# Splitting one attention mix around the next unit's logits in a gated attention and feed-forward kernel

## The chip, the core and the metric

The kernel runs on one core of a Trainium2 chip. The core has a matrix engine (TensorE, PE in the profile; its weight loads are PEld), a vector engine (VectorE, DVE), a scalar engine (ScalarE, ACT), a general engine (GpSimd, POOL) and a queue engine (SyncE, SP), and transfers (DMA) that SP, ACT and POOL issue. The metric is the time of one execution on the device in microseconds (us). Before the change three runs gave 593.22, 592.76 and 597.3 us, a median of 593.22.

## The reference

For 2048 tokens of 512 channels the kernel computes a gate g per token, an attention a, a feed-forward b, and g * a + (1 - g) * b. The attention has 32 heads of 16 channels; each token looks at 8 earlier ones, 2 apart.

```python
def _A_ref(x, wqkv, wo):
    H = 32; Dh = D // H; W, dil = 8, 2
    q, k, v = ...                       # x @ wqkv, by head
    idx = pos[:, None] - arange(W) * dil
    logits = einsum("bhsd,bhswd->bhsw", q, kg) * Dh ** -0.5   # masked where idx < 0
    attn = softmax(logits, axis=-1)
    o = einsum("bhsw,bhswd->bhsd", attn, vg)
    return o @ wo

def _B_ref(x, w_gate, w_up, w_down):
    return (gelu(x @ w_gate) * (x @ w_up)) @ w_down

g = sigmoid((x * gate_w).sum(-1, keepdims=True))
return g * a + (1 - g) * b
```

## The kernel before, in words

As the window has a step of 2, even and odd tokens never meet. The kernel does the even half (the first parity, `par` 0) and then the odd half (the second parity, `par` 1). For each parity it makes keys and queries, then values, and runs the feed-forward in 14 stages `f` (`ffn`, `gate_up`, `down`). All products are made on TensorE in single precision from pairs of a high and a low part, with block products saved by sums of operands (seven products in place of eight).

**Attention** is not on TensorE. A unit is 128 of the 512 channels (8 heads) of one parity, so there are four units for each parity, (0,0) to (0,3) and (1,0) to (1,3). For each unit VectorE does:
- `scores`: four times a product of queries and keys (tile `prod` from `kq`, L539) and its sum over a head's channels (L542) into the logits `lg`;
- `exps`: the maximum (L553), a subtraction (L555), and the exponential on ScalarE (L557);
- `shares`: the sum (L562), its reciprocal (L564), for the second parity the gate (L566), and a product (L568);
- `mix`: four times a product of the shares with the values (tile `v`, L585) and three additions (L589, L591, L593) into `o`, and after each second one a transposition (L598) into `tb`, whose four stores go to the DRAM tile `os` (L600, on SP).

**Loads.** `load_kq` fetches the keys and queries of a unit into the one buffer `kq`, `load_values` the values into the one buffer `v`, both on SP (L520, L523, L524). A load waits until the last product that reads the buffer is done.

**What sets the order.** `attention` is a generator that yields a number, an estimate of VectorE time, after each piece of work. The feed-forward calls `pull` with a budget between its products, and `pull` takes pieces off the generator until the budget is used. The pieces get a lower priority (`BEHIND`), and a scheduler then sets the final order of every engine's instructions, which the engines take in order. So a change to the order of pieces can move the instructions of all engines from that point on. From the fifth unit on (`i >= PIPE`, the second parity) the units are pipelined: between a unit's shares and its mix stand the next unit's logits and exponential.

**Feed-forward helpers on VectorE and ScalarE.** In each stage ScalarE copies products out of the banks `p` and `acc` of the accumulator memory (L786, L792, L845, L882, L898) and puts earlier sums back (L824, L867); VectorE adds (L793), multiplies (L797) and makes the low parts `hl` (L801). Four `p` banks serve in turn, so a product waits until its bank has been copied out.

**The end.** `out_first` multiplies the first parity's attention by the output weights (L1062, tile names `p_5354` and later). `finish` adds the second parity's: `channels` loads `os` into `raw` (L1040, SP), ScalarE casts the high part `hh` (L90), VectorE subtracts to make the low part `hl` (L91), TensorE adds the products for 4 units and 8 row groups (L1062) into `acc` and `p`, and copies on ScalarE (L1111) and VectorE (L1109) go to the output (L1115). The last pair is `hh_5673` and `hl_5674`.

Of the kernel before, what the change touches and what calls it, by code (L numbers as in the profile page):

```python
# [36 lines left out]
PIPE = 4  # L37
# [11 lines left out]
def tile_gated_mix(ctx: ExitStack, tc: tile.TileContext, xt, wqkv, wff, wo, out):  # L49
# [458 lines left out]
    def load_kq(par, u):  # L508
        hh, c = divmod(u, 2)
        kq = KQ.pop() if KQ else pool.tile([P, 3 * NP - 1, UC], F32, name="kq")  # L510
        k, q = kq[:, :2 * NP - 1], kq[:, 2 * NP - 1:]
        LG[par, u] = k, q
        if not (par or u):

            nc.gpsimd.memset(k[:1, :NP - 1], 0.0)
            for a, b in (1, P - 15), (P - 15, P):
                nc.sync.dma_start(k[a:b, :NP - 1], k[a - 1:b - 1, NP:])
            return
        load_slots(k, KS[par, hh][c], paced)
        paced(nc.sync.dma_start(q, QS[par, hh][c].rearrange("(p j) d -> p j d", j=NP)))  # L520
# [50 lines left out]
    VT = {}  # L571

    def load_values(par, u):
        hh, c = divmod(u, 2)
        VT[par, u] = v = pool.tile([P, 2 * NP - 1, UC], F32, name="v")
        load_slots(v, VS[par, hh][c])

    def mix(par, u):
        lg, v = LG.pop((par, u)), VT.pop((par, u))
        tb = pool.tile([P, 2, BT * UC], F32, name="tb")  # L580
        for jj in range(0, NP, 2):
            if jj % BT == 0:
                o = pool.tile([P, 4, BT, 32], F32, name="o")
            prod = pool.tile([P, 2, W, UC], F32, name="prod")
            paced(nc.vector.tensor_tensor(prod.rearrange("p j w (h d) -> p (j w) h d", d=DH),  # L585
                                          spans(v, jj).rearrange("p j w (h d) -> p j w h d", d=DH),
                                          two_of(lg, jj)[:, :, :, None].to_broadcast([P, 2 * W, UH, DH]), op=OP.mult))
            yield 2.3
            nc.vector.tensor_tensor(prod[:, :, :4], prod[:, :, :4], prod[:, :, 4:], op=OP.add)  # L589
            yield 1.2  # L590
            nc.vector.tensor_tensor(prod[:, :, :2], prod[:, :, :2], prod[:, :, 2:4], op=OP.add)  # L591
            two = [prod[:, :, i].rearrange("p j (b c) -> p b j c", b=4) for i in range(2)]
            nc.vector.tensor_tensor(o[:, :, jj % BT:jj % BT + 2], *two, op=OP.add)  # L593
            yield 1.1

            if jj % BT == BT - 2:
                t = tb[:, jj // BT]
                nc.vector.transpose(t, o.rearrange("p b t c -> p (b t c)"))  # L598
                for a in range(4):
                    nc.sync.dma_start(OS[par, u, jj // BT][:, :, a].rearrange("b i c -> i b c"),  # L600
                                      t[32 * a:32 * a + 32].rearrange("p (b c) -> p b c", b=4))
                yield 0.7

    done = set()
# [17 lines left out]
    def attention():  # L622
        units = [(0, u) for u in range(NU)] + [(1, u) for u in range(NU)]
        scored, ready, shared = [0], [], []

        def keyed(i):
            return i < len(units) and (units[i][0], units[i][1] // 2 * 2) in done

        def logits(i):
            if units[i] not in LG:  # L630
                load_kq(*units[i])
                yield LOAD
            yield from scores(*units[i])
            scored.append(i)

        yield from need(0, 0)
        yield from scores(0, 0)
        yield from need(0, 1)
        mixed = False
        for i, un in enumerate(units):  # L640
            if i not in scored:
                yield from need(un[0], un[1] // 2 * 2)
                yield from logits(i)
                mixed = False
            if i not in ready:
                if i >= PIPE and keyed(i + 1):
                    load_kq(*units[i + 1])
                yield from exps(*un)
            yield from need(un[0], 1)
            if i not in shared:  # L650
                yield from shares(*un)
            pipe, ahead = i >= PIPE and keyed(i + 1), i and keyed(i + 1)
            if not pipe and ahead:
                load_kq(*units[i + 1])
            load_values(*un)
            if pipe:
                yield from logits(i + 1)
                if keyed(i + 2):
                    load_kq(*units[i + 2])
                yield from exps(*units[i + 1])  # L660
                ready.append(i + 1)
            elif mixed:
                yield LOAD
            yield from mix(*un)
            done.add((*un, "o"))
            mixed = not ahead
            if pipe:
                yield from shares(*units[i + 1])
                shared.append(i + 1)
            elif ahead:  # L670
                yield from logits(i + 1)
# [684 lines left out]
```

## Time and profile before

| what | value |
|---|---|
| three times | 593.22, 592.76, 597.3 us |
| profiled execution, its own time | 592.89 us |
| its span, first to last instruction | 591.1 us |
| TensorE busy | 585.7 us (99%) |
| VectorE busy | 535.0 us (91%) |
| ScalarE busy | 425.3 us (72%) |
| granted TensorE clock, mean | 1.000 |

A row of the timeline has the start in us from the start of the span, the duration, the engine, the line, the operation, the tile written and the tile read, and in brackets the idle time ahead of it and what ended that. SPq is SP's queue: such a row is the issue of a transfer, not the transfer. A row of stretches has the stretch, its length, and the busy time and count of PE, PEld, DVE, ACT and POOL, then the granted clock, the share of the DMA engines and GB/s. A wait has the waiting instruction, what it waited for, the total, the count and the longest.

### The profile page before, as it was taken

What the parts mean: (1) busy time and instruction counts of PE and PEld (TensorE: products, weight loads), DVE (VectorE), ACT (ScalarE), POOL (GpSimd) and SP (SyncE); (2) the same over time, 40 slices, a digit from 0 to 9 for tenths busy, and PEclk for the clock granted to TensorE, in tenths of its full rate; (3) what the DMA queues carried; (4) which work ended last, traced back from release to release, by engine and by line L of the source; (5) the groups of instructions that cost most, each with busy time, mean ns of one, the idle gap of its engine ahead of it and who ended that gap; (6) DMA issues with size and microseconds to landing.
All of it is one profiled execution on the core that took longest, in us unless ns stands there. A gap on an engine that the chain in (4) does not pass through costs nothing.

```text
span 591.1 us, 8266 instructions
## 1 busy us (share of the span) xinstructions
PE 585.7 (99%) x2743; PEld 489.1 (83%) x2743; DVE 535.0 (91%) x628; ACT 425.3 (72%) x752; POOL 126.8 (21%) x153
## 2 busy tenths in 40 slices
PE   9999999999999999999999999999999999999997
PEld 7889888888888888888889888888888888887885
DVE  6989998999899995998997999998999899989882
ACT  6778667778887779786687655768776967796522
POOL 0140751112111212113120761112121212112200
PEclk9999999999999999999999999999999999999999
DMA  8789999978987979899989999969798989548915
GB/s 305 228 247 281 301 310 231 296 197 238 289 222 218 273 205 273 224 264 347 284 231 380 222 272 269 277 162 257 178 263 224 254 213 247 144 111 227 202 44 178
DMA packets 87848, 141.71 MB, mean 240 GB/s; under 512 B 8575, under 2 KB 49919, under 8 KB 87806
## 3 DMA queue, kind: packets, MB, share of 16 engines
q1 hardware_dynamic: 65454, 103.21, 52.2%
q0 software_dynamic: 22064, 37.59, 34.6%
q8 instruction: 21, 0.34, 0.2%
q10 hardware_dynamic: 288, 0.39, 0.2%
q14 instruction: 21, 0.17, 0.1%
HBM read 69.83 MB, written 46.49 MB: 197 GB/s over the span
## 4 chain that ended last, share of the span: by engine, by line
PE 96%; ACT 2%; DMA 1%; issue 0%; SPq 0%; DVE 0%; ACTq 0%
PE p L781 44%; PE p L830 13%; PE acc L830 12%; PE acc L478 11%; PE p L1062 6%; PE p L364 4%; PE acc L364 3%; PE p L478 2%; PE acc L1062 2%; DMA raw<-xt 1%; ACT A L90 0%; ACT L898 0%; ACT g L135 0%; ACT hl L805 0%; ACT hh L807 0%
## 5 line engine op out<-in xcount | busy, mean ns | idle before, releaser
L781 PE MATMUL p<-S,g 128*128 128x512 f32 x672 | 167.0, 389 | 0.0
L781 PEld LDWEIGHTS p<-S,g 128*128 128x128 f32 x672 | 125.8, 188 | 25.8
L781 PE MATMUL p<-A,g 128*128 128x512 f32 x504 | 125.8, 389 | 0.0
L781 PEld LDWEIGHTS p<-A,g 128*128 128x128 f32 x504 | 94.4, 188 | 19.8 <-ACT rt L845 0.4
L585 DVE TENSOR_TENSOR prod<-v,lg 128x2048 f32<-128x2048 f32 x32 | 72.8, 2274 | 1.4 <-DMA v<-vs 1.2
L542 DVE TENSOR_REDUCE lg<-prod 128x128 f32<-128x2048 f32 x32 | 73.0, 2280 | 0.2
L539 DVE TENSOR_TENSOR prod<-kq 128x2048 f32<-128x2048 f32 x32 | 72.9, 2277 | 0.2
L830 PE MATMUL p<-d,hh 128*128 128x512 f32 x224 | 68.6, 390 | 0.3 <-ACT p L824 0.3
L830 PE MATMUL acc<-d,hh 128*128 128x512 f32 x224 | 59.7, 389 | 0.0
L740 POOL DMA_DIRECT2D g<-raw x26 | 23.6, 907 | 161.1 <-ACT g L737 103.6
L792 ACT ACTIVATE c<-p 128x512 f32<-128x512 f32 x56 | 33.4, 597 | 33.7 <-PE p L781 33.6
L830 PEld LDWEIGHTS p<-d,hh 128*128 128x128 f32 x224 | 41.9, 188 | 9.5 <-ACT p L824 0.8
L830 PEld LDWEIGHTS acc<-d,hh 128*128 128x128 f32 x224 | 42.0, 188 | 8.7
L793 DVE TENSOR_TENSOR c<-c,s 128x512 f32<-128x512 f32 x56 | 37.8, 681 | 5.5 <-ACT c L792 5.2
L830 PE MATMUL p<-d,hl 128*128 128x512 f32 x112 | 42.1, 389 | 0.0
L797 DVE TENSOR_TENSOR c<-c 128x512 f32<-128x512 f32 x56 | 38.1, 683 | 1.3 <-ACT c L898 1.2
L589 DVE TENSOR_TENSOR prod<-prod 128x1024 f32<-128x1024 f32 x32 | 39.0, 1217 | 0.1
L845 ACT ACTIVATE rt<-p 128x512 f32<-128x512 f32 x48 | 27.8, 596 | 15.0 <-PE p L830 14.8
L786 ACT ACTIVATE s<-p 128x512 f32<-128x512 f32 x56 | 33.2, 594 | 5.3 <-PE p L781 4.9
L478 PE MATMUL acc<-d,S 128*128 128x512 f32 x144 | 35.5, 390 | 0.1
L830 PE MATMUL acc<-d,hl 128*128 128x512 f32 x112 | 35.1, 389 | 0.0
L772 POOL DMA_DIRECT2D d<-r x23 | 19.8, 860 | 68.9 <-ACT d L771 41.6
(222 smaller groups left out, 1062.3 us busy)
## 6 DMA issues: line engine op xcount, KB each, us to landing
g<-raw POOLq DMA_DIRECT2D x26, 512.0 KB, 6.7
ws<-g SPq DMA_DIRECT2D x14, 768.0 KB, 5.9
g<-ws SPq DMA_DIRECT2D x14, 768.0 KB, 6.7
r<-wff SPq DMA_DIRECT2D x28, 256.0 KB, 4.4
raw<-wff SPq DMA_DIRECT2D x14, 512.0 KB, 4.6
d<-r POOLq DMA_DIRECT2D x23, 256.0 KB, 6.7
ws<-raw SPq DMA_DIRECT2D x14, 384.0 KB, 5.8
raw<-ws SPq DMA_DIRECT2D x14, 384.0 KB, 4.0
```

The source lines that it names most:

```text
L364: LAST[:] = [nc.tensor.matmul(ps[:, :n], x[:, ts], VO[b][w][:, kc * WQ:kc * WQ + n], start=first, stop=(kc == 1 and i == 2), skip_group_ch ...
L478: LAST[:] = [nc.tensor.matmul(ps, x[:, ts], w, start=(start and kc == i == 0), stop=(kc == 1 and i == 2), skip_group_check=True)]
L539: paced(nc.vector.tensor_tensor(prod, spans(k, jj), q[:, jj:jj + 2, None, :].to_broadcast([P, 2, W, UC]), op=OP.mult))
L542: nc.vector.tensor_reduce(two_of(lg, jj), prod.rearrange("p j w (h d) -> p (j w) h d", d=DH), axis=AX.X, op=OP.add)
L585: paced(nc.vector.tensor_tensor(prod.rearrange("p j w (h d) -> p (j w) h d", d=DH), spans(v, jj).rearrange("p j w (h d) -> p j w h d", d=D ...
L589: nc.vector.tensor_tensor(prod[:, :, :4], prod[:, :, :4], prod[:, :, 4:], op=OP.add)
L781: LAST[:] = [nc.tensor.matmul(ps, w_, a_, start=(start and kc == 0 and n == 0), stop=(kc == 1 and n == 2), skip_group_check=True)]
L792: nc.scalar.activation(c, ps, AF.Copy)
L793: nc.vector.tensor_tensor(c, c, s, op=OP.add)
L797: nc.vector.tensor_tensor(ge, ge, up, op=OP.mult)
L830: LAST[:] = [nc.tensor.matmul(pp, a[:, ts], w, start=(i == 0 and n == 0 and gr == 0), stop=(i == 1 and n == 2), skip_group_check=True)]
L1062: LAST[:] = [nc.tensor.matmul(pa, a, b, start=(first and n == 0), stop=(last and n == 2), skip_group_check=True)]
```

## The change

In `mix`, each of the four quarters is entered in the set `done` once its additions are made. In `attention`, for the first unit of the second parity (`i == PIPE`), the mix is begun ahead of the next unit's logits, and stopped when its second quarter is done; the rest of it (the first transposition with its stores, the third and fourth quarter) follows behind the next unit's logits and exponential, where the whole mix stood. `load_values` of that unit is called ahead of `load_kq` of the next, and ahead of the unit's own exponential. The other units go as before. Nothing that is computed changes.

```diff
--- before.py
+++ after.py
@@ -591,6 +591,7 @@
             nc.vector.tensor_tensor(prod[:, :, :2], prod[:, :, :2], prod[:, :, 2:4], op=OP.add)
             two = [prod[:, :, i].rearrange("p j (b c) -> p b j c", b=4) for i in range(2)]
             nc.vector.tensor_tensor(o[:, :, jj % BT:jj % BT + 2], *two, op=OP.add)
+            done.add((par, u, jj))
             yield 1.1
 
             if jj % BT == BT - 2:
@@ -644,6 +645,7 @@
                 mixed = False
             if i not in ready:
                 if i >= PIPE and keyed(i + 1):
+                    load_values(*un)
                     load_kq(*units[i + 1])
                 yield from exps(*un)
             yield from need(un[0], 1)
@@ -652,8 +654,15 @@
             pipe, ahead = i >= PIPE and keyed(i + 1), i and keyed(i + 1)
             if not pipe and ahead:
                 load_kq(*units[i + 1])
-            load_values(*un)
+            if un not in VT:
+                load_values(*un)
+            steps = mix(*un)
             if pipe:
+                if i == PIPE:
+                    for c in steps:
+                        yield c
+                        if (*un, 2) in done:
+                            break
                 yield from logits(i + 1)
                 if keyed(i + 2):
                     load_kq(*units[i + 2])
@@ -661,7 +670,7 @@
                 ready.append(i + 1)
             elif mixed:
                 yield LOAD
-            yield from mix(*un)
+            yield from steps
             done.add((*un, "o"))
             mixed = not ahead
             if pipe:
```

Lines of the changed kernel from L594 on are 1 higher, and from L673 on 9 higher, than those of before (L793 becomes L802, L1109 becomes L1118).

VectorE, at the softmax of unit (1,0), before (`kq` is the keys of unit (1,1), `c` and `hl` belong to the feed-forward):

```order
L555 TENSOR_TENSOR lg<-lg,m 128x512
L539 TENSOR_TENSOR prod<-kq 128x2048
L562 TENSOR_REDUCE m<-lg 128x64
L542 TENSOR_REDUCE lg<-prod 128x16x8
L793 TENSOR_TENSOR c<-c,s 128x512
L564 RECIPROCAL m<-m 128x64
L793 TENSOR_TENSOR c<-c,s 128x512
L539 TENSOR_TENSOR prod<-kq 128x2048
L797 TENSOR_TENSOR c<-c 128x512
L566 TENSOR_TENSOR m<-m,g 128x64
L542 TENSOR_REDUCE lg<-prod 128x16x8
L797 TENSOR_TENSOR c<-c 128x512
```

VectorE at the same place, after the change:

```order
L555 TENSOR_TENSOR lg<-lg,m 128x512
L562 TENSOR_REDUCE m<-lg 128x64
L564 RECIPROCAL m<-m 128x64
L566 TENSOR_TENSOR m<-m,g 128x64
L568 TENSOR_TENSOR lg<-lg,m 128x512
L802 TENSOR_TENSOR c<-c,s 128x512
L585 TENSOR_TENSOR prod<-v,lg 128x2048
L806 TENSOR_TENSOR c<-c 128x512
L802 TENSOR_TENSOR c<-c,s 128x512
L589 TENSOR_TENSOR prod<-prod 128x2x512
L810 TENSOR_TENSOR hl<-c,hh 128x512
L591 TENSOR_TENSOR prod<-prod 128x2x256
```

The products of the next unit's logits (L539) and their sums (L542) have moved out; the sum of the softmax (L562) follows the subtraction (L555) directly, and the first product of the mix (L585) comes up.

TensorE in the last feed-forward stage, before (`p_5179` is a product of that stage, `p_5289` and `p_5324` take the last but one group of down products, `p_5354` is the first final product of `out_first`; `p_5354` has the bank that `p_5204`, another product of the stage, had):

```order
L830 MATMUL p_5289<-d_4827,hh_4963 128x512 x2
L830 MATMUL p_5289<-d_4827,hl_4964 128x512
L830 MATMUL p_5289<-d_4949,hh_5094 128x512 x2
L830 MATMUL p_5289<-d_4949,hl_5095 128x512
L781 MATMUL p_5179<-S_2942,g1_5106 128x512 x3
L781 MATMUL p_5179<-S_2957,g1_5106 128x512 x3
L830 MATMUL p_5324<-d_4827,hh_4963 128x512 x2
L830 MATMUL p_5324<-d_4827,hl_4964 128x512
L830 MATMUL p_5324<-d_4949,hh_5094 128x512 x2
L830 MATMUL p_5324<-d_4949,hl_5095 128x512
L1062 MATMUL p_5354<-g1_5191,A_5261 128x512 x3
L1062 MATMUL p_5354<-g1_5191,A_5282 128x512 x3
```

TensorE at the same place, after the change:

```order
L790 MATMUL p_5179<-S_2942,g1_5106 128x512 x3
L790 MATMUL p_5179<-S_2957,g1_5106 128x512 x3
L839 MATMUL p_5289<-d_4827,hh_4963 128x512 x2
L839 MATMUL p_5289<-d_4827,hl_4964 128x512
L839 MATMUL p_5289<-d_4949,hh_5094 128x512 x2
L839 MATMUL p_5289<-d_4949,hl_5095 128x512
L1071 MATMUL p_5354<-g1_5191,A_5261 128x512 x3
L1071 MATMUL p_5354<-g1_5191,A_5282 128x512 x3
L1071 MATMUL p_5354<-S_5237,A_5319 128x512 x2
L839 MATMUL p_5324<-d_4827,hh_4963 128x512 x2
```

The product into `p_5179` has moved ahead of `p_5289`, and most of `p_5354` ahead of `p_5324`. On ScalarE, at the same place, the copy that empties `p_5204` (into `c_5279`, L792, now L801) stood behind the one that fills `p_5324` (L824, now L833) and now stands ahead of it.

VectorE at the end of the program, before (`os`, `raw` and `hh_5673` carry the last attention output; `acc1`, `acc3`, `p_5571` and `p_5589` are final sums):

```order
L593 TENSOR_TENSOR o_5394<-prod_5416 128x4x64
L598 STREAM_TRANSPOSE tb_5301<-o_5394 128x512
L91 TENSOR_TENSOR hl_5674<-raw_5632,hh_5673 128x4x4x32
L1109 COPY rt_5704<-acc1_3744 128x512
L1109 COPY rt_5722<-acc3_3746 128x512
L1109 COPY rt_5734<-p_5571 128x512
L1107 COPY rt_5746<-p_5589 128x256
```

VectorE at the end, after the change:

```order
L593 TENSOR_TENSOR o_5394<-prod_5416 128x4x64
L599 STREAM_TRANSPOSE tb_5301<-o_5394 128x512
L1118 COPY rt_5704<-acc1_3747 128x512
L1118 COPY rt_5722<-acc3_3749 128x512
L91 TENSOR_TENSOR hl_5674<-raw_5632,hh_5673 128x4x4x32
L1118 COPY rt_5734<-p_5571 128x512
L1116 COPY rt_5746<-p_5589 128x256
```

The last subtraction L91, which makes `hl_5674`, stood ahead of the copies of `acc1` and `acc3` and now stands behind them. In SP's queue the last load of `raw` stood right behind the last stores of `os`; now the first output transfer (L1115, now L1124) stands between them. On ScalarE the copy of `acc2` stood behind the last cast L90 and now stands ahead of it.

## The prediction

> **What bounds the kernel now.** I read the page first, then who TensorE (PE) waits for, then stretches of the span, then the order of instructions in time around the moved work and at the end.
>
> ```profile
> span 591.1 us, 8266 instructions
> PE 585.7 (99%) x2743; PEld 489.1 (83%) x2743; DVE 535.0 (91%) x628; ACT 425.3 (72%) x752; POOL 126.8 (21%) x153
> ```
> ```profile
> PE p L76 <- DVE warm L73: 1.0, 1, 1.0
> PE p L830 <- ACT p L824: 0.3, 1, 0.3
> ```
> ```profile
> 380.00:576.00 196.00, 195.67 (x863) 161.70 (x862) 184.02 (x194) 140.92 (x235) 32.92 (x39) 1.00 0.77 195
> 576.00:592.00 16.00, 11.28 (x50) 9.01 (x48) 3.10 (x5) 3.41 (x6) 0.00 (x0) 0.99 0.46 164
> ```
>
> The page gives PE 99% of the span: 591.1 - 585.7 = 5.4 us idle in all. The waits of PE name two, 1.0 us at the start and 0.33 us once in the middle. From 380 to 576 us, where the changed work lies, PE is busy 195.67 of 196.00 us; VectorE (DVE), which carries the attention, is busy 184.02, so it has 12.0 us to spare there, and ScalarE (ACT) 55. Most of PE's other idle time is the last stretch, after its last matmul. So the change can give PE nothing beyond that 0.33 us; it can only give it new waits. DVE's time is worth something only where PE waits for it.
>
> That "99%" could hide slow matmuls, so I look at their spacing.
>
> ```profile
> 528.00 1.52 PE L781 MATMUL p<-S,g 128*128 128x512 f32 x6
> 529.36 0.62 PE L830 MATMUL p<-d,hh 128*128 128x512 f32 x2
> L781 PEld LDWEIGHTS p<-S,g 128*128 128x128 f32 x672 | 125.8, 188 | 25.8
> ```
>
> Six matmuls of 512 columns start within 529.36 - 528.00 = 1.36 us, 0.227 us apart, and a weight load takes 0.188 us, so 0.188/0.227 = 83% loading is what a PE without gaps shows here. The Trainium skill ("Perfetto Trace Analysis", Identifying the Most-Contended Engine) says that matmul busy time is a poor measure of the distance to the limit and that the weight loads' share should be read; by that rule 17% would be open. The rows above answer it: the 83% belongs to the shape.
>
> **The change part by part.** Computed work is the same: the same 628 DVE instructions, matmuls and DMAs. Only places move.
>
> *The values' load.* It is written ahead of the second unit's keys, but in SyncE's (SP's) queue it stood there before.
>
> ```profile
> 342.33 0.38 SPq L523 DMA_DIRECT2D v<-vs  x1
> 369.32 0.32 SPq L523 DMA_DIRECT2D kq<-ks  x1
> ```
> ```profile
> 403.67 2.27 DVE L585 TENSOR_TENSOR prod<-v,lg 128x2048 f32<-128x2048 f32 x1
> ```
>
> The values left at 342 us, the keys at 369, and the changed program has both at the same rows of SP. The values are now needed some 23 us before their first product at 403.67, at about 381 us, still over 30 us after their issue. Cost 0.
>
> *The first exponential.* Half of the mix now stands behind the unit's softmax without logits between.
>
> ```profile
> 376.28 0.68 DVE L555 TENSOR_TENSOR lg<-lg,m 128x512 f32<-128x512 f32 x1
> 376.88 2.29 DVE L539 TENSOR_TENSOR prod<-kq 128x2048 f32<-128x2048 f32 x1
> 379.08 0.68 DVE L562 TENSOR_REDUCE m<-lg 128x64 f32<-128x512 f32 x1
> ```
> ```profile
> 377.79 0.63 ACT L557 ACTIVATE lg<-lg 128x512 f32<-128x512 f32 x1
> ```
>
> Before, one product of logits (2.29 us) filled the time that the exponential needs on ACT. Now the sum L562 stands right behind L555: DVE waits from 376.28 + 0.68 = 376.96 to 377.79 + 0.63 = 378.42, **+1.5 us** of DVE.
>
> *The second exponential* gains what the first loses:
>
> ```profile
> 411.55 0.69 DVE L562 TENSOR_REDUCE m<-lg 128x64 f32<-128x512 f32 x1 [2.22 <-ACT lg L557]
> 465.58 0.69 DVE L562 TENSOR_REDUCE m<-lg 128x64 f32<-128x512 f32 x1 [1.66 <-ACT lg L557]
> ```
>
> In the changed order a 2.3 us product of the mix and two 0.68 us additions stand between L555 and L562, beside the two short additions that were there. The 2.22 us wait goes, **-2.2 us**. The third and fourth keep about the same company as before (0).
>
> *The feed-forward's vector instructions.* Summing the attention rows ahead of the same feed-forward row in both orders, at 0.5 to 2.2 us each, gives 0 to 4.9 us less ahead of it in the changed order, nowhere more than 0.4 us more until the last rows. So PE's own helpers on DVE (L793, L797, L801) come earlier and hold PE up nowhere; but DVE's queue is taken in order, and where such a row comes before its operand from ACT, DVE waits and the attention behind it slips. Bounds: nothing (PE's pace leaves the 12.0 us) and 4.9 us (the whole distance waited out once). I take **+2 us**, since the waits of this kind that before shows are 0.3 to 1 us each and a few are added. DVE ends the attention later by d = 1.5 - 2.2 + 2 = 1.3 us, between -0.7 and 4.2. The last transposition has room for that, see below.
>
> *The stores of the first half mix* now stand in SP's queue ahead of a load of r and of a weight load:
>
> ```profile
> 397.32 0.33 SPq L702 DMA_DIRECT2D r<-wff  x1
> 404.38 0.64 ACT L771 ACTIVATE d<-r 128x512 fp32r<-128x512 f32 x1
> ```
> ```profile
> r<-wff SPq DMA_DIRECT2D x28, 256.0 KB, 4.4
> ```
> ```profile
> 399.68 0.33 SPq L523 DMA_DIRECT2D kq<-ks  x1
> ```
> ```profile
> 433.72 2.25 DVE L539 TENSOR_TENSOR prod<-kq 128x2048 f32<-128x2048 f32 x1
> ```
> ```profile
> DMA to landing us min/median/max: 3.0/5.8/11.4
> ```
>
> The transposition comes at about 396, so three stores of some 0.45 us delay that load by about 1.5 us; it lands in 4.4 us, about 403, and is used at 404.4. The keys of the third unit go out after the later logits, near 415 instead of 400, and are needed at 434; they land in 5.8 us as a median, 11.4 at most (the last row is of kq's tile). The POOL queue's transfers follow ACT as before. Cost 0; without these covers 1 to 2 us once.
>
> *The last gate of the feed-forward.* PE's order changes here: the first final product p_5354 now stands ahead of p_5324, and its bank is that of p_5204.
>
> ```profile
> 532.57 0.72 PE L830 MATMUL p<-d,hh 128*128 128x512 f32 x2 [0.33 <-ACT p L824]
> ```
> ```profile
> 531.91 0.61 ACT L824 ACTIVATE p<-rt 128x512 f32<-128x512 f32 x1
> 532.43 0.60 ACT L792 ACTIVATE c<-p 128x512 f32<-128x512 f32 x1
> ```
>
> PE is free at 532.57 - 0.33 = 532.24. Before it waited for the copy L824; now it waits for the copy L792 that frees p_5204's bank, at 532.43 + 0.60 = 533.03 before. On ACT one copy (0.52 us) has moved behind it, which would give 532.5, but the fourth exponential's table loads and two casts stand nearer, which costs up to 1.1 us. So the wait is 0.3 to 1.4 us in place of 0.33. I take 533.1, 0.85 us: **+0.5 us**, between 0 and 1.0.
>
> *The end.* This is the place where DVE is on PE's path.
>
> ```profile
> 575.20 0.71 DVE L598 STREAM_TRANSPOSE tb<-o 128x512 f32<-128x512 f32 x1
> 582.53 0.69 DVE L91 TENSOR_TENSOR hl<-raw,hh 128x512 fp32r<-128x512 f32 x1 [6.62 <-ACT hh L90]
> 583.14 0.68 DVE L1109 COPY rt<-acc 128x512 f32<-128x512 f32 x1
> 584.60 0.69 DVE L1109 COPY rt<-acc 128x512 f32<-128x512 f32 x1 [0.78 <-PE acc L1062]
> ```
> ```profile
> 584.17 0.39 PE L1062 MATMUL acc<-S,hl 128*128 128x512 f32 x1
> 584.40 0.62 PE L1062 MATMUL p<-S,hh 128*128 128x512 f32 x2
> 584.86 0.39 PE L1062 MATMUL p<-S,hl 128*128 128x512 f32 x1
> ```
> ```profile
> 579.16 0.34 SPq L1040 DMA_DIRECT2D raw<-os  x1
> 581.14 0.36 SPq L1115 DMA_DIRECT2D out<-s  x1
> ```
> ```profile
> 581.87 0.63 ACT L90 ACTIVATE hh<-raw 128x512 fp32r<-128x512 f32 x1 [0.75 <-DMA raw<-os]
> 583.24 0.60 ACT L1111 ACTIVATE s<-acc 128x512 f32<-128x512 f32 x1 [0.74 <-PE acc L1062]
> ```
>
> Before, the last subtraction L91 makes hl_5674 by 582.53 + 0.69 = 583.22, and PE reads it first at 584.86: 1.64 us to spare. In the changed program L91 stands behind both copies L1109 (there L1118), and the second copy waits for the matmul at 584.17. It starts at 584.60, and as the next DVE instruction follows 0.61 us after one of this shape (583.14 - 582.53), L91 starts at 585.21 and ends at 585.90. PE reads hl_5674 then instead of at 584.86: **+1.04 us**, and the rest of the end follows PE. Two more queues are turned round: SP issues the last load of raw behind the first output, at 581.14 + 0.36 = 581.50, so ACT's cast starts 581.87 - 579.16 = 2.71 us after that, at 584.21, and could feed L91 at 584.87; ACT's cast stands behind the copy at 583.24 (free at 583.84). Both end ahead of 585.21 and cost nothing more. A later attention adds only from d = 585.21 - 582.53 = 2.7 us on; at the bound of 4.2 it adds 1.5.
>
> **Sum**, against the profiled execution's 592.89 us (span 591.1 and 1.8 around it; the three times' median, 593.22, is 0.33 higher): 592.89 + 0.5 + 1.04 = 594.4.
>
> **The rivals.**
> - *Hidden.* If ACT is ahead in the last gate and PE's wait there goes, and the tail is run through with less than its 1.04 us, nothing is left: 592.89 - 0.33 = 592.6. For it speaks that PE was fed almost everywhere; against it that the tail's wait hangs on one queue's order.
> - *Slower: the feed-forward waits recur.* If the 2 us of DVE waits come again in each of the three units that follow, d = 1.3 + 3 x 2 = 7.3, and L91 starts at 582.53 + 7.3 = 589.83: PE waits 589.83 + 0.69 - 584.86 = 5.7 us, with 0.5 before it 592.89 + 6.2 = 599.1. It decides over 1% (5.9 us) from about this d on. For it: DVE is at 94% between 380 and 576. Against: 12.0 us spare, and waits in before of this kind are under 1 us, as PE paces both. The granted clock was 1.00 to 576 and 0.99 behind it. The Trainium skill ("TensorE: Matmul & The Clock Gate", The HAM clock gate) says that an idle window of about 3.4 us halves PE's clock; no wait between matmuls in this trace is long enough to show it. By it such a wait would also slow the last ten matmuls, 2.3 us at the spacing above, an estimate of 2.3 us more.
> - *Faster: the filled 2.2 us moves the end forward.* PE has 0.33 us to gain before its last matmul; over 1% would need more than the 5.4 us idle in all. At best 592.5.
> - *The change does not do what it says:* half of it doesn't, the values' load has its old place. If the scheduler's new order as a whole came out equal, 592.9.
>
> **How the numbers follow.** Forecast 0.68; hidden 0.14; slower 0.09; faster 0.01 (for what I can't see); no effect 0.08. Predicted is the forecast's 594.4. The range starts at 592.4 (hidden, less the 0.13 by which the lowest time before lies under the profiled one) and reaches 597.3: 592.89 + 1.0 + 1.04 + 1.5 = 596.4, and 0.9 towards the slower case, which is left out with its 0.09. Faster by over 1%, the least that a measurement of this kernel can tell from no change: 0.01; within 1%: 0.90; slower by over 1%: 0.09.
>
> **What would show it.** DVE: a wait of about 1.5 us at the first L562 of the moved unit and none at the second. PE: a wait for a copy of ACT near 532 us, and one of about 1 us for DVE ahead of the last ten matmuls, with the second copy L1118 just before the last L91. PE busy unchanged at 585.7. It is wrong if PE waits for DVE or ACT anywhere between 380 and 530 us, or if the last transposition comes more than 2.7 us later than 575.2.

## The result and the profile after

The changed kernel took 596.46 us as a median of 22 runs (595.54 to 598.87), the kernel before 593.05 us beside it (22 runs). The ratio (of the means) is 1.0052, with a 95% interval of 1.0039 to 1.0065: slower by about half a per cent, 3 us. That is within 1%, as forecast, and inside the range (592.4 to 597.3), but the sum had only 594.4. The profiled execution took 595.89 us, against 592.89 before, so 3.0 us more where the sum had 1.5.

The page of the changed kernel, first rows, and the waits of PE:

```profile
span 594.1 us, 8264 instructions
PE 587.3 (99%) x2743; PEld 489.5 (82%) x2743; DVE 535.5 (90%) x628; ACT 425.8 (72%) x752; POOL 126.7 (21%) x153
```
```profile
PE p L1071 <- ACT hh L90: 1.1, 1, 1.1
PE p L76 <- DVE warm L73: 1.0, 1, 1.0
PE p L1071 <- ACT c L801: 0.3, 1, 0.3
PE p L790 <- ACT s L795: 0.2, 1, 0.2
PE acc L839 <- DMA hl<-c: 0.2, 1, 0.2
```

The 0.3 us for `c` of L801 stands where 0.3 us for L824 stood. New are three: 1.1 us for a cast at the end, 0.2 us for the copy L795, 0.2 us for a transfer of `hl`. They sum to 1.5 us, and the span grew by 3.0. The rest appears when the same matmul is looked up in both traces (2743 in each, taken in order of start). From 20 us after the start up to 437 us the difference is 0.13 us at most. Then it grows in four steps, worked out from the starts: 0.46 us at 437, 0.40 at 523, 0.50 at 528 (together 1.35, with rounding; the gate at 533 is even) and 1.65 at the end.

The first step. Rows of before, then of the changed kernel, around 427 us on ACT, and PE's matmul:

```profile
427.83 0.62 ACT L805 ACTIVATE hl<-c 128x512 fp32r<-128x512 f32 x1
428.75 0.86 POOL L806 DMA_DIRECT2D hl<-c  x1 [6.72 <-ACT hl L805]
437.33 0.84 PE L830 MATMUL acc<-d,hl 128*128 128x512 f32 x3
```
```profile
426.63 1.28 ACT L557 ACT_TABLE_LOAD   x1
427.93 0.63 ACT L557 ACTIVATE lg<-lg 128x512 f32<-128x512 f32 x1
429.46 0.62 ACT L814 ACTIVATE hl<-c 128x512 fp32r<-128x512 f32 x1
430.38 0.86 POOL L815 DMA_DIRECT2D hl<-c  x1 [9.47 <-ACT hl L814]
437.67 0.96 PE L839 MATMUL acc<-d,hl 128*128 128x512 f32 x3 [0.17 <-DMA hl<-c]
```

The exponential of unit (1,1) now lies on ACT just ahead of a feed-forward copy. Its table takes 1.28 us, the next instruction starts 0.54 us after the exponential, and the feed-forward product `hl` that POOL transfers goes out 430.38 - 428.75 = 1.63 us later. The matmul that needs it starts some 7.3 us after the issue, at 437.67; before, it started at 437.33, so 0.33 us are lost there. (The row shows only 0.17 us of idle time, as the matmul ahead is recorded with 0.39 us, though the next one can start 0.227 us after it.) Another 0.11 us of the step come right behind: the next matmul starts 0.337 us after this one in place of 0.227. The kernel before has the same number of table loads, 18; the one of this exponential stood at 409.59 us there, and PE waited for nothing behind it. The chain that ended last (start, length, what) passes through this transfer, and at the end through the last load:

```profile
430.38 7.24 DMA hl<-c
...
583.33 2.90 DMA raw<-os
```

The steps at 523 and 528 come behind the exponential of (1,3), whose table load started at 518.46 us before. Rows of the changed kernel (the first wait stands at the weights, PEld):

```profile
520.83 1.28 ACT L557 ACT_TABLE_LOAD   x1
522.66 0.58 ACT L876 ACTIVATE p<-p 128x512 f32<-128x512 f32 x1
523.30 1.23 PEld L790 LDWEIGHTS p<-S,g 128*128 128x128 f32 x6 [0.54 <-ACT p L876]
525.89 1.28 ACT L907 ACT_TABLE_LOAD   x1
527.68 0.59 ACT L795 ACTIVATE s<-p 128x512 f32<-128x512 f32 x1
528.33 1.67 PE L790 MATMUL p<-S,g 128*128 128x512 f32 x6 [0.20 <-ACT s L795]
```

The last rows on which PE waits, in the changed kernel:

```profile
578.94 0.71 DVE L599 STREAM_TRANSPOSE tb<-o 128x512 f32<-128x512 f32 x1
582.49 0.36 SPq L1124 DMA_DIRECT2D out<-s  x1
583.33 0.34 SPq L1049 DMA_DIRECT2D raw<-os  x1
585.95 0.69 DVE L1118 COPY rt<-acc 128x512 f32<-128x512 f32 x1 [2.03 <-PE acc L1071]
586.32 0.63 ACT L90 ACTIVATE hh<-raw 128x512 fp32r<-128x512 f32 x1 [1.13 <-DMA raw<-os]
586.98 0.69 DVE L91 TENSOR_TENSOR hl<-raw,hh 128x512 fp32r<-128x512 f32 x1 [0.34 <-ACT hh L90]
587.00 0.73 PE L1071 MATMUL p<-S,hh 128*128 128x512 f32 x2 [1.08 <-ACT hh L90]
587.72 0.19 PEld L1071 LDWEIGHTS p<-S,hl 128*128 128x128 f32 x1 [0.43 <-DVE hl L91]
```

The last transposition comes at 578.94 in place of 575.20, 3.74 us late. PE would have been at the row of 587.00 at 584.40 + 1.35 = 585.75, so it waits 1.25 us for the cast, not for the subtraction. The next three matmuls follow 0.34, 0.39 and 0.34 us apart in place of 0.227, which makes 0.40 us more, 1.65 in all. The middle one of these is a second wait: that matmul reads `hl`, and its weights wait for the subtraction, which ends at 586.98 + 0.69 = 587.67 (the last row).

### The profile page after: what moved, and what is told of

It reads as the page before. It is cut to its first block, busy times and chain, and to the rows that moved or that the text cites. A ratio compares the mean times of both kernels' runs of the same rounds, so it can differ in the third digit from the quotient of the medians.

```text
span 594.1 us, 8264 instructions
## 1 busy us (share of the span) xinstructions
PE 587.3 (99%) x2743; PEld 489.5 (82%) x2743; DVE 535.5 (90%) x628; ACT 425.8 (72%) x752; POOL 126.7 (21%) x153
## 4 chain that ended last, share of the span: by engine, by line
PE 92%; ACT 3%; issue 2%; DMA 2%; POOL 0%; DVE 0%; SPq 0%; ACTq 0%; POOLq 0%
PE p L790 41%; PE p L839 12%; PE acc L839 12%; PE acc L478 11%; PE p L1071 5%; PE p L364 4%; PE acc L364 3%; PE p L478 2%; PE acc L1071 1%; DMA hl<-c 1%; PE p L76 1%; DMA raw<-os 0%; ACT A L90 0%; ACT L907 0%; ACT L557 0%
## 5 line engine op out<-in xcount | busy, mean ns | idle before, releaser
L585 DVE TENSOR_TENSOR prod<-v,lg 128x2048 f32<-128x2048 f32 x32 | 72.8, 2276 | 4.1 <-DMA v<-vs 3.8
L539 DVE TENSOR_TENSOR prod<-kq 128x2048 f32<-128x2048 f32 x32 | 72.9, 2279 | 0.4
L542 DVE TENSOR_REDUCE lg<-prod 128x128 f32<-128x2048 f32 x32 | 73.0, 2281 | 0.2
L801 ACT ACTIVATE c<-p 128x512 f32<-128x512 f32 x56 | 33.4, 597 | 35.7 <-PE p L790 35.6
L802 DVE TENSOR_TENSOR c<-c,s 128x512 f32<-128x512 f32 x56 | 38.0, 682 | 5.4 <-ACT c L801 5.2
L806 DVE TENSOR_TENSOR c<-c 128x512 f32<-128x512 f32 x56 | 38.2, 683 | 2.9 <-ACT c L907 2.9
L795 ACT ACTIVATE s<-p 128x512 f32<-128x512 f32 x56 | 33.2, 594 | 7.7 <-PE p L790 7.4
L839 PE MATMUL acc<-d,hl 128*128 128x512 f32 x112 | 36.4, 390 | 0.2 <-DMA hl<-c 0.2
```

Of the source, the lines that this page charges most:

```text
L539: paced(nc.vector.tensor_tensor(prod, spans(k, jj), q[:, jj:jj + 2, None, :].to_broadcast([P, 2, W, UC]), op=OP.mult))
L542: nc.vector.tensor_reduce(two_of(lg, jj), prod.rearrange("p j w (h d) -> p (j w) h d", d=DH), axis=AX.X, op=OP.add)
L801: nc.scalar.activation(c, ps, AF.Copy)
L802: nc.vector.tensor_tensor(c, c, s, op=OP.add)
L806: nc.vector.tensor_tensor(ge, ge, up, op=OP.mult)
L839: LAST[:] = [nc.tensor.matmul(pp, a[:, ts], w, start=(i == 0 and n == 0 and gr == 0), stop=(i == 1 and n == 2), skip_group_check=True)]
```

## The experiments

Two questions were open: what makes the 1.65 us at the end (the turned order of the queues, the late transposition, or both), and what makes the steps (the table loads, or the moved accumulations). In the tables "steps" is PE's lateness against before at 580 us less that at 370 us (which the start of the program moves by up to 0.7 us from one execution to the next), "at the end" is what the last matmul adds to that, and "transposition" how late the last one is, all from the profiled execution. Line numbers of these kernels differ by a few from those above.

### The order at the end and the lateness, apart and together

Four kernels. `behind(x, y)` orders x behind y on its engine; `ENDS` holds the last load, cast and subtraction. The changed kernel with the old order at its end:

```diff
-                nc.vector.tensor_copy(r, pa)
+                behind(nc.vector.tensor_copy(r, pa).ins, ENDS["low"].ins.name)
...
+                if jj:
+                    behind(ins.ins, ENDS["cast"].ins.name)
...
+                if not jj:
+                    behind(ins.ins, ENDS["load"].ins.name)
```

> Cover: the 1.65 us at the end of the changed kernel have two limits that lie one beneath the other, the lateness of the last transposition (3.74 us, of which PE's own lateness of 1.35 us hides a part) and the turned order (the last subtraction behind the copy of the fourth accumulator). With the old order alone the lateness is left: the raw load leaves about 582.9, the cast ends about 586.25 against a want of 585.75, the subtraction about 586.95 against 586.2, so PE waits 0.75 us in place of 1.65, and the time is 0.9 us less than the changed kernel's, 2.1 us over before. Queue alone (the turned order makes all of it): 1.65 us less than the changed kernel. Lateness alone (the order costs nothing): no change from the changed kernel.

The kernel before with the new order at its end:

```diff
+                if jj < BT:
+                    behind(ENDS["low"].ins, ins.ins.name)
...
+                if jj == 2:
+                    behind(ENDS["cast"].ins, ins.ins.name)
...
+                if not jj:
+                    behind(ENDS["load"].ins, ins.ins.name)
```

> The kernel before with the changed kernel's order at the very end, and nothing else: the last subtraction behind the copies of the second and fourth accumulator, the first store of the output ahead of the last raw load, the third accumulator's copy ahead of the last cast. Cover: the subtraction starts when the fourth accumulator's copy ends, 585.29, and ends 585.98 against a want of 584.86, so before plus 1.1 us. Queue alone: before plus 1.65 us. Lateness alone: before plus 0 to 0.4 us (the cast behind the store).

The kernel before, held to its own order at the end by the lines of the first edit, with a late transposition:

```diff
-            nc.vector.tensor_tensor(o[:, :, jj % BT:jj % BT + 2], *two, op=OP.add)
+            for _ in range(7 if (par, u, jj) == (1, NU - 1, NP - 2) else 1):
+                nc.vector.tensor_tensor(o[:, :, jj % BT:jj % BT + 2], *two, op=OP.add)
```

> The kernel before, in its own order, with the last addition of the last unit's mix made seven times in place of once (six times 0.43 us, so the last transposition 2.5 to 2.6 us later, the lateness of the changed kernel less PE's own). Cover: the raw load leaves about 581.7, the cast ends about 585.0 against a want of 584.40, the subtraction about 585.75 against 584.86, so before plus 0.9 us. Queue alone: before plus 0. Lateness alone: before plus 1.65 us.

The kernel before with both edits:

> The kernel before with both: the order of the changed kernel's end and the last addition made seven times. Cover: before plus 1.4 to 1.7 us, as much as the changed kernel loses there, and less than the sum of the two alone (2.0). Queue alone and lateness alone: before plus 1.65 us. If the two were to add, before plus 2.0 us.

| kernel | steps | transposition, less PE's own lateness | PE's wait at the end | at the end | ratio to before |
|---|---|---|---|---|---|
| changed | 1.35 | 2.39 | 1.25 | 1.65 | 1.0052 (1.0039 to 1.0065) |
| changed, old order at the end | 2.00 | 2.39 | 0.77 | 1.20 | 1.0048 (1.0016 to 1.0080) |
| before, new order | - | 0.36 | 1.06 | 1.46 | 1.0037 (1.0004 to 1.0070) |
| before, late | 0.01 | 3.15 | 1.52 | 1.92 | 1.0029 (1.0000 to 1.0057) |
| before, new order and late | - | 2.57 | 1.46 | 1.86 | 1.0043 (1.0016 to 1.0070) |

The profiled executions of the two kernels "before, new order" are among their longest (601.35 and 601.88 us, medians 595.01 and 595.61): PE pauses in them around 391 and 410 us, 6.8 and 6.9 us in all, at places that the edit does not touch, so their end is read against PE's own time.

Rows of the end of "before, new order":

```profile
588.15 0.36 SPq L1122 DMA_DIRECT2D out<-s  x1
588.98 0.34 SPq L1040 DMA_DIRECT2D raw<-os  x1
591.61 0.69 DVE L1112 COPY rt<-acc 128x512 f32<-128x512 f32 x1 [2.03 <-PE acc L1065]
591.78 0.63 ACT L1044 ACTIVATE hh<-raw 128x512 fp32r<-128x512 f32 x1 [0.94 <-DMA raw<-os]
592.47 0.73 PE L1065 MATMUL p<-S,hh 128*128 128x512 f32 x2 [0.90 <-ACT hh L1044]
```

Queue alone and lateness alone both fall: each of the two makes PE wait by itself, 1.06 and (with 2.39 us of lateness) 0.77 us, and together they make 1.25, far from the sum of 1.83. That is the reading called cover. In the new order the raw load leaves 0.47 us after the end of the output's issue (588.98 - 588.15 - 0.36), and the output waits for PE's sums, so this path goes with PE and not with the transposition. In the changed kernel the same gap stands, 583.33 - 582.49 - 0.36 = 0.48, so there, too, the output set the load free. The transposition is only just behind it: in "new order and late", where it decides, the load leaves 4.28 us after the transposition's start, which would be 583.22 in the changed kernel. So in the changed kernel the turned order makes the wait, and the lateness lies covered beneath it. The 0.19 us by which 1.25 exceeds 1.06 are the transfer's: from the load's issue to the cast it took 586.32 - 583.33 = 2.99 us, in "new order" 591.78 - 588.98 = 2.80. In "new order and late" it took 3.12, which is 0.32 of the 0.40 us over "new order"; what makes it longer stays open.

What was mis-sized in the expectations: the added lateness of "before, late" came out as 3.15 us, not 2.55 (0.39 of it as the values of the last unit were waited for 1.64 us in place of 1.25), and behind each wait for the cast stand 0.4 us more, the wait for the subtraction and two slower starts, which none of the sums had. The first of the four lies no lower than the changed kernel as a whole, since its steps were 0.65 us larger in the profiled execution; in the runs the two can't be told apart.

### Exponentials left out

The exponential of unit (1,1), of (1,3), or of both is left out and a copy made in its place; no table is loaded for them, and nothing else moves.

```diff
-        nc.scalar.activation(lg, lg, AF.Exp, scale=DH ** -0.5)
+        nc.scalar.activation(lg, lg, AF.Copy if (par, u) == (1, 1) else AF.Exp, scale=DH ** -0.5)
```

> The changed kernel with the exponential of unit (1,1) left out (the logits are copied in its place), so that ScalarE loads no table for it; the order of every engine is the changed kernel's. Table: PE's first step of 0.46 us at 437 us and VectorE's wait of 1.68 us at 434.0 come from the two table loads of 1.3 us there, and go; the lateness of the last transposition falls by about 1.3 us, which the end gives back in part: 0.5 to 1.5 us less than the changed kernel. Order: the steps come from the moved accumulations, stay, and the time is the changed kernel's within 0.2 us.

> The changed kernel with the exponential of unit (1,3) left out in the same way. Table: PE's steps of 0.40 us at 523 and 0.50 us at 528 go, the last transposition comes about 1 us sooner: 0.9 to 1.9 us less than the changed kernel. Order: both steps stay, and the time is the changed kernel's within 0.2 us.

> The changed kernel with both exponentials left out, those of (1,1) and (1,3). Table: no step is left before the end; the lateness of the last transposition is 1 to 1.5 us and the raw load waits for the first store instead; the turned order is left, so before plus 1.1 us. Order: before plus 2.5 to 3 us. Had the turned order cost nothing, before plus 0 to 0.4 us.

> The kernel before with the same two exponentials left out: what leaving them out gains where nothing was moved. Table: PE waits for nothing there, so before within 0.3 us. If leaving them out makes the kernel faster by 1 us or more here too, the gain of the other three says nothing on the change.

| kernel | step at 437 | steps at 523 and 528 | steps, all | transposition | at the end | ratio to before |
|---|---|---|---|---|---|---|
| changed | 0.46 | 0.89 | 1.35 | 3.74 | 1.65 | 1.0052 (1.0039 to 1.0065) |
| without (1,1) | 0.00 | 0.89 | 0.89 | 3.28 | 1.65 | 1.0044 (1.0021 to 1.0066) |
| without (1,3) | 1.05 | 0.00 | 0.41 | 3.34 | 1.98 | 1.0032 (1.0017 to 1.0048) |
| without both | 0.00 | 0.00 | -0.64 | 3.44 | 4.74 | 1.0028 (1.0006 to 1.0050) |
| before without both | 0.00 | 0.00 | -0.64 | -1.16 | 0.00 | 1.0009 (0.9979 to 1.0040) |

Each step goes with its exponential and stays with the other's, though the order of the accumulations is the same in all: the steps are the table loads', at the places to which the new order brings them, and the reading called order falls. (The -0.64 is the wait at 533 us, 0.33 in its row and 0.49 in the starts, with the slower start behind it, which also goes.) But the second half of what was expected failed. With both left out, the transposition stays 3.44 us late, PE comes earlier, and the end takes it back. Rows of the kernel without both:

```profile
579.08 0.71 DVE L599 STREAM_TRANSPOSE tb<-o 128x512 f32<-128x512 f32 x1
586.97 0.73 PE L1071 MATMUL p<-S,hh 128*128 128x512 f32 x2 [2.61 <-ACT hh L90]
```

That execution is the longest of its 11 runs (597.3 us; four lie at 593.87 to 594.91, seven at 595.73 to 597.30), so 4.74 us is not what each of them loses; the transposition's place is read from the profile. The mean granted clock is 0.999 or 1.0 in the four and 0.996 or 0.997 in the seven, so the fall of the clock that the last section shows is in most of them, and in the ratio.

VectorE's lateness is thus not carried from wait to wait. Without (1,1) the wait of 1.68 us at 434 went, and the mix of (1,0) ended only 1.46 us late in place of 3.20. One unit further on most of that was gone: the third exponential's sum waited 2.75 us in place of 2.24, and came 0.5 us sooner (468.52, with the 0.14 by which that program starts earlier, against 469.13):

```profile
434.01 0.69 DVE L806 TENSOR_TENSOR c<-c 128x512 f32<-128x512 f32 x1 [1.68 <-ACT c L907]
469.13 0.69 DVE L562 TENSOR_REDUCE m<-lg 128x64 f32<-128x512 f32 x1 [2.24 <-ACT lg L557]
```
```profile
468.52 0.69 DVE L562 TENSOR_REDUCE m<-lg 128x64 f32<-128x512 f32 x1 [2.75 <-ACT lg L557]
```

The first fence is the changed kernel, the second the one without (1,1). The last place where VectorE is held is the values of the last unit: the one buffer is free when the unit before has read it.

```profile
549.80 0.34 SPq L523 DMA_DIRECT2D v<-vs  x1
556.79 2.29 DVE L585 TENSOR_TENSOR prod<-v,lg 128x2048 f32<-128x2048 f32 x1 [3.83 <-DMA v<-vs]
```
```profile
557.49 2.29 DVE L585 TENSOR_TENSOR prod<-v,lg 128x2048 f32<-128x2048 f32 x1 [5.21 <-DMA v<-vs]
```

The first fence is the changed kernel again, the second the one without both: what the exponentials gave, this wait took. Before, the load left at 546.40 and the wait was 1.25 us.

### The last unit's values early

The next theory: the late values make the transposition late. They get the buffer of the keys, which is free after the last logits, and so leave ahead of the last unit's exponential. In the two kernels made from the changed one the scheduler also turned part of the end back: the last raw load stands ahead of the output again, the last cast ahead of the third accumulator's copy, and the last subtraction ahead of one of the two copies. So their ends are not those of early values alone.

```diff
-        VT[par, u] = v = pool.tile([P, 2 * NP - 1, UC], F32, name="v")
+        if (par, u) == (1, NU - 1):
+            v = pool.tile([P, 3 * NP - 1, UC], F32, name="kq")[:, :2 * NP - 1]
+        else:
+            v = pool.tile([P, 2 * NP - 1, UC], F32, name="v")
+        VT[par, u] = v
...
+                elif units[i + 1] == (1, NU - 1):
+                    load_values(*units[i + 1])
```

> The changed kernel with the values of the last unit loaded into the buffer of the keys, which no unit needs any more, ahead of that unit's exponential, in place of the one buffer of values, which is free only when the unit before has read it. Chain (the end of the changed kernel is the last transposition plus 7.6 to 8.1 us, and the transposition is late because VectorE waits 3.83 us for these values; the steps on PE before it are hidden under that): the wait goes, the last transposition comes 3.8 us sooner, at about 575.1, PE waits for nothing at the end, and only the steps of 1.35 us are left: before plus 1.2 to 1.5 us, about 1.6 less than the changed kernel. If the lateness came from elsewhere: the time of the changed kernel within 0.3 us.

> The same with the exponentials of (1,1) and (1,3) left out. Chain: neither a step nor a wait at the end is left, so the time of before with both left out, that is before minus 0.6 to plus 0.3 us; leaving them out is worth 1.3 us or more here, where without the early values it was worth nothing. If the steps are set by the order of the accumulations: before plus 1.2 to 1.5 us.

> The kernel before with the same early values. Chain: its last transposition comes 1.2 us sooner, which nothing waits for: before within 0.3 us. If the load's time matters to PE in some other way (its transfers collide with those of the output weights or of the feed-forward), before plus or minus 0.5 us or more.

| kernel | steps | transposition | at the end | ratio to before |
|---|---|---|---|---|
| changed, early values | 2.03 | 3.93 | 0.94 | 1.0065 (1.0052 to 1.0079) |
| the same without both exponentials | -0.64 | 1.19 | 0.89 | 1.0003 (0.9989 to 1.0018) |
| before, early values | 0.01 | -0.52 | 0.00 | 1.0038 (1.0013 to 1.0062) |

The first expectation failed. VectorE's wait for the values is gone, and the transposition is as late as it was. Three other waits stand in its place, 1.28, 1.07 and 1.28 us (VectorE's rows of this kernel):

```profile
538.93 0.69 DVE L91 TENSOR_TENSOR S<-raw,S 128x512 fp32r<-128x512 f32 x1 [1.28 <-ACT S L90]
562.84 0.69 DVE L91 TENSOR_TENSOR hl<-raw,hh 128x512 fp32r<-128x512 f32 x1 [1.07 <-ACT hh L90]
573.11 0.69 DVE L91 TENSOR_TENSOR hl<-raw,hh 128x512 fp32r<-128x512 f32 x1 [1.28 <-ACT hh L90]
578.94 0.71 DVE L603 STREAM_TRANSPOSE tb<-o 128x512 f32<-128x512 f32 x1
```

They are subtractions of the output stage that stand between the steps of the mix. Ahead of the first and the last, ACT's cast waited for a load of `os`:

```profile
538.26 0.63 ACT L90 ACTIVATE S<-raw 128x512 fp32r<-128x512 f32 x1 [1.88 <-DMA raw<-os]
572.45 0.63 ACT L90 ACTIVATE hh<-raw 128x512 fp32r<-128x512 f32 x1 [4.09 <-DMA raw<-os]
```

The same three stand in the kernel without both exponentials (0.60, 1.71 and 1.21 us, 3.52 in all, against 3.63), where the transposition comes 2.7 us sooner. So they are not what makes the difference.

The second expectation held: with the early values, leaving the exponentials out brings the last matmul 2.7 us forward (steps and end 2.97 before, 0.25 after it) and the ratio from 1.0065 to 1.0003. Nearly all of that are the steps, 2.03 and -0.64; the end stays at 0.9, and it does not grow as it did with the late values. By the ratios, the early values alone take nothing off the changed kernel's 1.0052 (they add 0.0013), the exponentials alone 0.0024, and both together 0.0049: more than the sum, though the order at the end and the fall of the clock are in these differences too. By the transposition it is plainer: 3.74 us late as changed, 3.93 and 3.44 with one of them, 1.19 with both. So it has two causes, each of which hides the other: the exponentials' table loads and the one buffer of values. On the third, the profile shows PE as in before (0.01 us), yet its runs lie 0.38% above. Four of the 12, at 597.19 to 600.76 us, make most of it; the other eight have a mean of 593.47. Where the four lose it stays open. None of the kernels that compute everything came out faster than before.

### A shorter last unit

```diff
+            if (par, u, jj) != (1, NU - 1, NP - 2):
                 nc.vector.tensor_tensor(prod[:, :, :4], prod[:, :, :4], prod[:, :, 4:], op=OP.add)
```

and the same ahead of the product and of the next addition.

> The changed kernel with the product and the first two foldings of the last unit's last pair of queries left out (2.29, 1.22 and 0.69 us; the pair before is added in their place), so that the last transposition comes about 4.8 us sooner, at 574.1, and with it the order at the end falls back to that of before. End (what is lost at the end comes from the lateness of the last transposition, whatever makes it late, and hides no more than PE's own steps): PE waits for nothing at the end, the steps of 0.46, 0.40 and 0.50 us stay, and the time is before plus 1.2 to 1.5 us, some 1.6 less than the changed kernel. If the end is set by something that does not follow the transposition: the time of the changed kernel within 0.3 us. If the steps are not PE's own but follow the end: before within 0.3 us.

The last pair's product and two foldings are left out. The order at the end falls back to that of before, PE waits for nothing there, the steps stay (1.93 us in this execution, 1.03 of it at 437), and the last matmul is 1.93 us late. The ratio is 1.0015 (0.9997 to 1.0034), and of its 12 runs the median is 595.07, 1.19 us above the kernel before beside it (593.88), about as expected. The transposition was still 1.15 us late against before, as the values came even later, but that is within what the old order hides (VectorE's rows of this kernel):

```profile
560.33 2.29 DVE L586 TENSOR_TENSOR prod<-v,lg 128x2048 f32<-128x2048 f32 x1 [4.96 <-DMA v<-vs]
577.00 0.71 DVE L602 STREAM_TRANSPOSE tb<-o 128x512 f32<-128x512 f32 x1
```

So the steps are PE's own and do not follow from the end. The size at 437 us is not settled to better than 0.46 to 1.13 us: it hangs on when one transfer lands, and the five profiled executions that have that step gave 0.46, 1.03, 1.05, 1.11 and 1.13. The profiled execution of the changed kernel has the smallest, and its 595.89 us lie 0.57 below the median of the runs.

## Why the prediction was right, and what its sum lacked

The time lay in the range, and on the side that was forecast, in part by luck. The range reached 597.3 by 1.0 us for the last gate and 1.5 us for a late transposition, which added nothing that shows; what was lost beside the turn stood in the sum at nothing. Both of its own signs of being wrong came: PE waited for ACT at 523 and 528 us, and the transposition came 3.74 us late, more than 2.7.

- **PE has nothing to gain.** Held. PE is busy 587.3 us where it was 585.7, with 2743 matmuls in both; the 1.6 us more are for the most part the slower starts behind waits, and the part of each wait that the recorded matmul ahead of it covers.
- **The values' load costs 0.** Held: its place among SP's rows is the old one, and no row of the moved unit waits for values.
- **First exponential +1.5, second -2.2.** Held. The rows of the changed kernel:

```profile
378.46 0.69 DVE L562 TENSOR_REDUCE m<-lg 128x64 f32<-128x512 f32 x1 [1.49 <-ACT lg L557]
429.45 0.68 DVE L562 TENSOR_REDUCE m<-lg 128x64 f32<-128x512 f32 x1
```

- **Feed-forward waits +2, d = 1.3.** Too small. The waits of L802 and L806 between 376 and 437 us are 0.33, 0.88, 0.81 and 1.68, 3.70 in all; before there was one, 0.67. That is 3.03 more, which with +1.5 and -2.2 makes 2.3; the unit ended 3.20 us late, and 0.9 us of that is in no named wait. I had reckoned with copies of ACT that come a little late, not with a copy that has two table loads ahead of it. The last transposition was 3.74 us late, inside the bounds (-0.7 to 4.2) but not by adding up: the wait for the last unit's values took its place.
- **Nowhere does the feed-forward hold PE up (0).** This step failed. I asked whether VectorE's rows come in time and let ACT's stand; but the exponential also moved on ACT, where its table loads push feed-forward copies back by 1.6 us. Two exponentials gave PE three new waits, 1.35 us. The prediction had named this as what would make it wrong.
- **The last gate +0.5.** Measured 0: the wait for L801 is 0.3 us as the one for L824 was. The order that I feared there cost nothing.
- **The turn at the end +1.04.** The wait was 1.06 us by itself in the kernel before, with 0.40 us behind it that the sum lacked. That the two sizes agree is luck, as the path was not the one I worked out. I had the raw load leave at 581.50, right behind the output's issue, and the cast feed L91 at 584.87, ahead of the copies. The load left 0.47 us after the end of that issue, and the cast (0.63 us from 591.78) ended just behind the second copy (0.69 from 591.61). PE waited for the cast: it reads `hh` at 584.40, ahead of `hl` at 584.86, and I had priced only `hl`. The subtraction came right behind it, as the second wait, of 0.16 us.
- **A later attention adds only from 2.7 us on.** Held as far as it was tried: at 3.74 us, of which PE's own lateness covers 1.35, the load left when the output let it. With 2.57 us of lateness ("new order and late") it left 0.08 us later against PE (588.96 - 6.90 for 588.98 - 7.00).
- **The rivals.** The slower one named waits that recur in each unit, d = 7.3. They do not: the last transpositions of the four units come 3.20, 3.54, 1.72 and 3.74 us late, where 2 us more in each were feared. The hidden one and no effect fall with the 3 us. Of the slower one's clock: the Trainium skill ("TensorE: Matmul & The Clock Gate", The HAM clock gate) has the clock halved after an idle window of about 3.4 us; the wait of 2.61 us in the kernel without both exponentials is shorter, and the clock fell all the same, as the last section shows.

The sum of what the profile shows: 1.35 (steps) + 1.25 (wait at the end) + 0.40 (the second wait and the slower starts behind it) = 3.00 us. Of this the sum on record had the turn (1.04) and put 0.5 at a place that cost nothing.

## What to carry to other kernels

When an attention step is moved, follow it on every engine that it uses: here 1.35 of the 3.0 us came from ScalarE, where two exponentials brought their table loads in front of copies that TensorE needs, and 1.65 from the order into which the scheduler put the very end. Look for the second path before a wait is priced: the turned queue and the late transposition, and the table loads and the single buffer, each hid the other, so that taking away one moved little: the old order at the end left 0.77 of 1.25 us, and the transposition came 0.3 us sooner or no sooner at all. A difference of 0.5% is found by laying the same matmul of two traces side by side, not in the shares of busy time, which stayed at 99%.

## What the runs showed of the hardware

- A wait of PE costs more than itself. Behind waits of 0.2 to 1.5 us the first matmul was followed after 0.335 to 0.341 us in place of 0.227, 0.11 us more each time, and the ones after it were 0.23 to 0.24 us apart again unless they waited anew.
- Behind a wait of 2.61 us it was more. Stretches of the kernel without both exponentials, with the granted clock third from the end:

```profile
576.00:584.00 8.00, 8.00 (x37) 6.57 (x35) 4.38 (x7) 1.20 (x2) 0.00 (x0) 1.00 0.21 66
584.00:588.00 4.00, 1.39 (x5) 0.60 (x4) 1.38 (x2) 0.63 (x1) 0.00 (x0) 0.96 0.84 264
588.00:592.00 4.00, 3.83 (x10) 2.67 (x9) 0.69 (x1) 1.33 (x3) 0.00 (x0) 0.61 0.33 129
```

  The 0.61 is a mean: the granted clock was 0.50 from 587.69 to 591.10 us and 1.00 on both sides. Six matmuls started 0.43 us apart in it, and the time lost behind the wait came to 2.0 us. Behind waits of 3.21 and 3.22 us (the pauses at 410 us in the two kernels "before, new order") the clock was 0.50 for 3.41 us as well; behind the 1.36 us of "before, late" it stayed at 1.00.
- The load of the last unit's values took 6.1 us from its issue to the first product in the kernel before, 7.0 in the changed one and 8.4 in the one without both exponentials, though the bytes are the same.
